# Pooled attention followed by a maxout feed-forward: third buffers for q, folds of v by four heads, prologue constants in later buffers, and a new order of all steps

## The chip, the cores and the metric

The kernel runs on one core of one Trainium2 chip. The core has TensorE (PE; its weight loads are shown as PEld), VectorE (DVE), ScalarE (ACT), GpSimd (POOL) and SyncE (SP). Each takes its instructions in the order in which the program issues them and waits at an instruction until the semaphores that it needs have been raised. The metric is the device time of one execution in microseconds (us); less is better. Three runs of the kernel before gave 227.71, 229.46 and 230.1 us, median 229.46.

## The reference

```python
# q, k, v: (8, 8, 576, 64) float32: batch, heads, sequence, head size
k_p = k.reshape(B, H, 72, 8, D).mean(axis=3)        # keys and values averaged over 8 neighbours
v_p = v.reshape(B, H, 72, 8, D).mean(axis=3)
scores = q @ k_p^T / sqrt(D)                        # 576 x 72 for each batch and head
attn = softmax(scores)
attn_out = attn @ v_p                               # (8, 8, 576, 64)
x = attn_out.transpose(0, 2, 1, 3).reshape(4608, 512)
h = max(max(x @ w1, x @ w2), x @ w3)                # 4608 x 768
out = h @ w_out                                     # 4608 x 512, float32
```

## The kernel before

**Tiling.** The attention goes batch by batch (8 batches b of 576 tokens, 8 heads), the feed-forward part by blocks n of 512 tokens (9 blocks). The transposed attention output is a ring `xT` of 2048 tokens, from which the blocks read, so that both parts run interleaved.

**Attention.** `load_q`, `load_k` and `load_v` (lines 89 to 115) load a batch from GpSimd's DMA queue into the pool `ld`, which has two buffers of each tile (`qb`, `ktFalse`, `vt`). Keys are pooled on VectorE in two additions (`pieces`, "k", lines 794 to 802; tiles `halfh`, `kp`) and turned by TensorE into `kz` (`turn_k`, line 207; `kz` is copied from PSUM by `move`). Values are folded in `pieces` (lines 803 to 814): four additions on GpSimd from `vt` into `half` (line 807, two heads each), two from `half` back into `vt` (line 811, four heads each), and one on VectorE into `vp`. q of batches 0 to 2 is transposed on TensorE (`turn_q`, line 187) and copied out of PSUM into `qT`; that of batches 3 to 7 by three DMA transposes on SyncE's queue (line 305). `scores_flat` (line 237) makes 512 columns of scores in a PSUM bank (`psf`, two of them) and ScalarE writes the exponentials to `et`. `values` (line 267) multiplies 128 tokens with `vp` into `pav` (one buffer), and VectorE divides by the sum (`rcp`, then `xn`, line 279). `turn_x` (line 250) brings `xn` into `xT`: for batches 0 to 2 through TensorE and PSUM, later by DMA transposes on SyncE's queue (line 256).

**Feed-forward.** The maximum of three products is written as max(x(w2-w1), x(w3-w1), 0) plus x w1, so that x w1 w_out becomes x times a matrix `wm` made once. Blocks 0 to 3 make plain products (`hidden`, `project`, `two_products`). For blocks 4 to 8 the hidden products, and for all blocks from 1 on the output products, are done in the form of seven half-size products for eight; they need sums of quarters on VectorE (`sum_t` and `sum_h`, line 596: tiles `xs`, `hs`; `fold_w` and `fold_out` for the weights: `sums`, `sw`, `soh`) and additions of the results (`hidden_product`, `out_product`). Results go through four PSUM banks `pb`, handed out by `take` and `give`. `move` (line 78) copies PSUM on ScalarE, or on VectorE where the step's name ends in a star. Stores go out on SyncE's queue (lines 421 and 692), those of the last block also on other queues.

**Order.** After a prologue (up to about 39 us in the profile) all is issued by `run` (line 829) from the string `ORDER` (line 879), step by step. The names: `qbi` transposes a part of q of batch b on TensorE, `Tb` issues the next of three DMA transposes of q, `sbj` makes a block of scores, `vbc` the values of 128 tokens (from batch 3 on with their transposes), `xbc` the transposes of batches 1 and 2, `Kb` and `Vb` the next piece of a fold, `kb` turns the keys, `<kb`, `<qb`, `<vb` load; `p` is a half of a first output tile; `f F S G` sums of weights, `t1..t4` and `u1..u4` sums of quarters; `A1..H4` plain hidden products; `1a..7c` hidden products and `1d..7d` output products of the seven.

Two additions of waits shape the queues. A load (`<`) waits for the latest matmul issued before it and for the latest DMA transpose issued before it (line 841). A GpSimd piece of a fold (`piece`, line 816) waits for the latest VectorE operation that was made through `both` (line 536), that is, one that works on SBUF alone.

Of the kernel before, what the change touches and what calls it, by code (L numbers as in the profile page):

```python
# [10 lines left out]
ALU = mybir.AluOpType  # L11
# [3 lines left out]
def kernel(  # L15
# [91 lines left out]
                for h, g in zip(cuts, cuts[1:])][-1]  # L107

    def load_q(b):
        qbs[b] = ld.tile([128, 4, NG, D], BF16, name="qb", tag="qb")  # L110
        src = q[b].rearrange("h s d -> (h s d)").rearrange(
            "(hp p t d) -> p hp t d", hp=4, p=128, t=NG)
        n = 2 if b == 0 else 4
        return [nc.gpsimd.dma_start(out=qbs[b][:, i:i + n], in_=src[:, i:i + n])
                for i in range(0, 4, n)][-1]
# [10 lines left out]

    load_q(0)
    load_k(0, nc.sync, F32, 3)
    warm = const.tile([128, 512], BF16, name="warm", tag="warm")
    nc.vector.memset(warm, 1.0)  # L130
    ident = const.tile([128, 128], BF16, name="ident", tag="ident")
    make_identity(nc, ident)
    identh = const.tile([128, 128], F16, name="identh", tag="identh")
    make_identity(nc, identh)
    load_v(0, nc.gpsimd, cuts=(0, 4, 8))
    pick = const.tile([96, 6, 128], F16, name="pick", tag="pick")
    nc.gpsimd.memset(pick, 1.0)
    for sign in (1, -1):
        nc.gpsimd.affine_select(
# [47 lines left out]

    def turn_q(b, n0, n1, evac, tag):
        if b not in qTs:
            qTs[b] = sb2.tile([128, 2 * NG, 128], BF16, name="qT", tag="qT")  # L190
        pqt = psum([128, n1 - n0, 128], BF16, name="pqt", tag=tag[0],
                       bufs=tag[1])
        qf = qbs[b].rearrange("p hp t d -> p (hp t d)")
        for n in range(n0, n1):
            transpose(pqt[:, n - n0, :], qf[:, 128 * n:128 * n + 128],
                                ident)
        evac(out=qTs[b][:, n0:n1, :], in_=pqt)
# [96 lines left out]
    def do(b, steps):  # L294

        for name in steps.split():
            i = int(name[1:] or 0)
            if name[0] == "q":  # L300
                turn_q(b, *QS[i], move, TR if len(pools) < 3 else SC)
            elif name[0] == "T":
                if i == 0:
                    qTs[b] = sb2.tile([128, 2 * NG, 128], BF16, name="qT", tag="qT")
                turned[:] = [nc.sync.dma_start_transpose(
                    out=qTs[b][:, 6 * i:6 * i + 6],
                    in_=qbs[b].rearrange("p hp t d -> p (hp t d)")[:, 768 * i:768 * i + 768])]
# [291 lines left out]

    def sum_h(n, i):  # L600
        if n not in ths:
            ths[n] = hs if n < LAST else const.tile([128, 4, JH, HALF], F16, name="hs8",
                                                    tag="half")
        sum_t(quads(n), ths[n], i)

    def bank(of, n, g):
# [184 lines left out]
    def pieces(what, b):  # L791

        t = (kts if what == "k" else vts)[b]
        if what == "k":
            new_kp(b)
            f = const.tile([96, 6, 4, D], F16, name="halfh", tag="k16")
            both(f, t[:, :, 0:4, :], t[:, :, 4:8, :], ALU.add)
            yield
            both(kps[b].rearrange("p j i d -> p i j d"), f[:, :, 0:2, :], f[:, :, 2:4, :],
                 ALU.add)  # L800
            yield
            return
        f = const.tile([Sp, H, 4, D], F32, name="half", tag="half")
        e = nc.gpsimd
        for i in range(0, H, 2):
            c = slice(i, i + 2)
            yield e.tensor_tensor(out=f[:, c], in0=t[:, c, 0:4, :], in1=t[:, c, 4:8, :],  # L807
                                  op=ALU.add)
        for i in range(0, H, 4):
            c = slice(i, i + 4)  # L810
            yield e.tensor_tensor(out=t[:, c, 0:2, :], in0=f[:, c, 0:2, :], in1=f[:, c, 2:4, :],  # L811
                                  op=ALU.add)
        both(vp_all[:, b % 3, :, 0:D], t[:, :, 0, :], t[:, :, 1, :], ALU.add)
        yield

# [84 lines left out]

    run(ORDER)
# [36 lines left out]
```

## Time and profile before

| | |
|---|---|
| Runs | 227.71, 229.46, 230.1 us; median 229.46 |
| The profiled execution | 227.75 us, span 225.9 us |
| TensorE clock granted, mean | 0.997 |
| DMA packets | 33.57 MB, mean 149 GB/s |
| 63 exponentials (ACT et<-psf) | 595 ns each |
| 28 first additions of v (POOL half<-vt) | 1189 ns each |
| 14 second additions of v (POOL vt<-half) | 1300 ns each |
| 40 divisions (DVE xn<-pav,rcp) | 691 ns each |
| Loads of q, k, v to landing, median | 9.5, 13.2, 14.1 us |

The page of the profile divides the span in 40 slices of 5.6 us; each digit is the busy share of an engine in a slice, in tenths:

```
PE   7788999899999999999998999996999999999991
DVE  3558967276999899987899965989989998988651
ACT  2267525687866887354369855957454571674230
POOL 7975300969419546459012027125140000000020
DMA  6999999989999799989999999995371541430085
```

In the rows of a timeline a line has start, duration, engine, line of the kernel, operation, out<-in and the count, and in brackets the idle time before it with what ended it. In the chain of waits a line has start, duration and the engine and tile that the end of the span depended on at that time.

### The profile page before, as it was taken

The numbers are of one execution on the slowest core, as the hardware profiler recorded it, in microseconds if no ns is written. First come the engines' busy times: TensorE is split into PE (matmuls) and PEld (weight loads), VectorE is DVE, ScalarE is ACT, GpSimd is POOL, SyncE is SP. The second block draws the span as 40 slices with busy tenths as digits, with TensorE's granted clock in tenths as the row PEclk, the third lists the DMA queues.
The fourth block names the chain that finished last, engine by engine and source line by source line (L and its number), as shares of the span: only waits on it lengthen the run. The fifth ranks groups of instructions, "written<-read, shape, count | busy, mean of one in ns | idle before, by whom it ended". The sixth has DMA issues, their size and how long they took to land.

```text
span 225.9 us, 5235 instructions
## 1 busy us (share of the span) xinstructions
PE 212.3 (94%) x2046; PEld 165.7 (73%) x2046; DVE 180.2 (80%) x362; ACT 132.0 (58%) x264; POOL 82.7 (37%) x90
## 2 busy tenths in 40 slices
PE   7788999899999999998999996999999999999991
PEld 2377745558986666874679885988989898888881
DVE  3558967276999899987899965989989998988651
ACT  2267525687866887354369855957454571674230
POOL 7975300969419546459012027125140000000020
PEclk9999999999999999999999999999999999999998
DMA  6999999989999799989999999995371541430085
GB/s 166 208 197 197 204 207 205 204 160 236 151 156 132 126 163 182 151 171 194 134 211 172 155 125 171 195 156 107 70 166 36 136 105 31 115 73 0 4 229 141
DMA packets 50824, 33.57 MB, mean 149 GB/s; under 512 B 27280, under 2 KB 46352, under 8 KB 50800
## 3 DMA queue, kind: packets, MB, share of 16 engines
q0 software_dynamic: 20304, 16.98, 51.6%
q1 hardware_dynamic: 30208, 16.00, 40.8%
q8 instruction: 16, 0.26, 0.5%
q10 hardware_dynamic: 288, 0.26, 0.4%
q14 instruction: 8, 0.07, 0.1%
HBM read 34.60 MB, written 9.44 MB: 195 GB/s over the span
## 4 chain that ended last, share of the span: by engine, by line
PE 73%; DVE 11%; DMA 9%; issue 3%; ACT 1%; POOL 1%; SPq 0%; POOLq 0%; DVEq 0%; ACTq 0%
PE pb L70 54%; PE psf L70 5%; DMA qT<-qb 5%; PE pw L70 4%; PE pav L70 4%; DMA vt<-in_v_dram 4%; DVE xn L279 3%; PE pm L70 2%; PE pxt L74 1%; DVE hT L682 1%; DVE xs L537 1%; PE oC L70 1%; DVE kz L78 1%; DVE hs L537 1%; DVE rcp L277 1%
## 5 line engine op out<-in xcount | busy, mean ns | idle before, releaser
L70 PE MATMUL pb<-xT,mw 128*128 128x256 f16 (+1 forms) x312 | 52.8, 305 | 1.2 <-DVE hT L682 1.2
L70 PEld LDWEIGHTS <-mw 128*128 128x128 f16 x444 | 41.5, 98 | 16.3 <-issue 2.2
L807 POOL TENSOR_TENSOR half<-vt 72x512 f32<-72x512 f16 x28 | 32.9, 1189 | 52.9 <-DMA vt<-in_v_dram 42.6
L226 ACT ACTIVATE et<-psf 72x512 f16<-72x512 f32 x63 | 35.3, 595 | 8.2 <-PE psf L70 8.1
L279 DVE TENSOR_TENSOR xn<-pav,rcp 128x512 f16<-128x512 f32 x40 | 27.7, 691 | 1.4
L78 ACT COPY osb<-pb 128x512 f32<-128x512 f32 x25 | 14.7, 587 | 23.7 <-PE pb L70 23.7
L70 PE MATMUL psf<-qT,kz 128*128 128x256 bf16 (+4 forms) x161 | 21.3, 249 | 2.6 <-DMA qT<-qb 2.0
L636 DVE TENSOR_TENSOR ys<-ys,pb 128x512 f16<-128x512 f16 x30 | 20.3, 682 | 2.3 <-PE pb L70 2.0
L70 PEld LDWEIGHTS <-kz 128*128 128x128 bf16 x185 | 14.6, 98 | 8.5 <-issue 3.4
L70 PEld LDWEIGHTS <-hs 128*128 128x128 f16 x192 | 18.8, 98 | 2.2
L811 POOL TENSOR_TENSOR vt<-half 72x512 f16<-72x512 f32 x14 | 18.0, 1300 | 5.9 <-DVE xs L537 3.4
L692 POOL DMA_DIRECT2D out_dram<-ob x2 | 1.3, 636 | 50.1 <-DVE ob L763 50.1
L70 PE MATMUL pb<-mwo,hT 128*128 128x256 f16 (+1 forms) x120 | 19.3, 294 | 0.0
L70 PE MATMUL pb<-soh,hs 128*128 128x256 f16 x138 | 19.1, 273 | 0.0
L70 PEld LDWEIGHTS <-hT 128*128 128x128 f16 x168 | 16.3, 98 | 3.6
L78 ACT COPY pb<-pb 128x512 f32<-128x512 f32 x21 | 12.0, 575 | 10.8 <-PE pb L70 7.0
L70 PE MATMUL pav<-vp,et 72*128 72x65 f16 x320 | 17.1, 194 | 0.8 <-DVE xn L279 0.4
L78 ACT CAST ys<-pb 128x512 f16<-128x512 f32 x27 | 15.6, 593 | 3.6 <-PE pb L70 3.3
L70 PE MATMUL pb<-xs,sums 128*128 128x256 f16 x90 | 17.2, 272 | 0.1
L70 PEld LDWEIGHTS <-et 72*128 72x128 f16 x320 | 14.6, 98 | 3.5 <-DVE xn L279 1.4
L70 PE MATMUL pb<-xs,sw 128*128 128x256 f16 x90 | 17.2, 272 | 0.0
L645 ACT ACTIVATE t<-pb 128x256 f16<-128x256 f32 x30 | 11.2, 387 | 8.2 <-PE pb L70 7.8
(111 smaller groups left out, 413.0 us busy)
## 6 DMA issues: line engine op xcount, KB each, us to landing
out_dram<-osb SPq DMA_DIRECT2D x38, 128.0 KB, 2.7
ktFalse<-in_k_dram POOLq DMA_DIRECT2D x7, 576.0 KB, 13.2
qb<-in_q_dram POOLq DMA_DIRECT2D x7, 576.0 KB, 9.5
vt<-in_v_dram POOLq DMA_DIRECT2D x7, 576.0 KB, 14.1
out_dram<-osb SPq DMA_DIRECT2D x13, 256.0 KB, 3.7
mw<-in_moe_w_dram POOLq DMA_DIRECT2D x9, 256.0 KB, 9.5
ktTrue<-in_k_dram SPq DMA_DIRECT2D x3, 384.0 KB, 5.5
mwo<-in_moe_w_out_dram POOLq DMA_DIRECT2D x1, 768.0 KB, 13.3
```

The lines of the kernel that those rows point to most:

```text
L70: latest[0] = nc.tensor.matmul(*args, **kw)
L74: latest[0] = nc.tensor.transpose(*args, **kw)
L78: (nc.vector.tensor_copy if on_vector[0] else nc.scalar.copy)(out=out, in_=in_)
L226: nc.scalar.activation(out=out, in_=in_, func=FT.Exp, scale=1.0 / 64.0)
L277: nc.vector.reciprocal(out=rcp, in_=pv[:, :, :, 64])
L279: nc.vector.tensor_tensor(out=xn, in0=pv[:, :, :, 0:D], in1=rcp.to_broadcast([128, 2, 4, D]), op=ALU.mult)
L537: t = e.tensor_tensor(out=out, in0=a, in1=b, op=op)
L636: nc.vector.tensor_tensor(out=y[:, j], in0=y[:, j], in1=bank("C", n, g), op=ALU.add)
L645: nc.scalar.activation(out=t0, in_=p[:, 0], func=FT.Relu)
L682: nc.vector.tensor_tensor(out=hTs[n][:, j, c], in0=relus[j], in1=b, op=ALU.max)
L807: yield e.tensor_tensor(out=f[:, c], in0=t[:, c, 0:4, :], in1=t[:, c, 4:8, :], op=ALU.add)
L811: yield e.tensor_tensor(out=t[:, c, 0:2, :], in0=f[:, c, 0:2, :], in1=f[:, c, 2:4, :], op=ALU.add)
```

## The change

Five things change.

- `qb` and `qT` have three buffers instead of two.
- `warm` and `pick`, constants of the prologue, are no longer in the pool `const`; they take a buffer of `t0` and of `kp`, which later steps use.
- `half`, the intermediate tile of the folds of v, holds four heads instead of eight. The six GpSimd additions of a batch are the same in kind and number; their order becomes two first additions, one second, two first, one second.
- `hs8`, the sums of the last block, was in the buffer of `half` and is now in one of `vt`.
- `ORDER` is new throughout. It has the same steps; six of the copies out of PSUM are starred that were not, and two no longer are.

```diff
--- before.py
+++ after.py
@@ -107,7 +107,7 @@
                 for h, g in zip(cuts, cuts[1:])][-1]
 
     def load_q(b):
-        qbs[b] = ld.tile([128, 4, NG, D], BF16, name="qb", tag="qb")
+        qbs[b] = ld.tile([128, 4, NG, D], BF16, name="qb", tag="qb", bufs=3)
         src = q[b].rearrange("h s d -> (h s d)").rearrange(
             "(hp p t d) -> p hp t d", hp=4, p=128, t=NG)
         n = 2 if b == 0 else 4
@@ -126,14 +126,14 @@
 
     load_q(0)
     load_k(0, nc.sync, F32, 3)
-    warm = const.tile([128, 512], BF16, name="warm", tag="warm")
+    warm = sb2.tile([128, 512], BF16, name="warm", tag="t0")
     nc.vector.memset(warm, 1.0)
     ident = const.tile([128, 128], BF16, name="ident", tag="ident")
     make_identity(nc, ident)
     identh = const.tile([128, 128], F16, name="identh", tag="identh")
     make_identity(nc, identh)
     load_v(0, nc.gpsimd, cuts=(0, 4, 8))
-    pick = const.tile([96, 6, 128], F16, name="pick", tag="pick")
+    pick = sb2.tile([96, 6, 128], F16, name="pick", tag="kp")
     nc.gpsimd.memset(pick, 1.0)
     for sign in (1, -1):
         nc.gpsimd.affine_select(
@@ -187,7 +187,7 @@
 
     def turn_q(b, n0, n1, evac, tag):
         if b not in qTs:
-            qTs[b] = sb2.tile([128, 2 * NG, 128], BF16, name="qT", tag="qT")
+            qTs[b] = sb2.tile([128, 2 * NG, 128], BF16, name="qT", tag="qT", bufs=3)
         pqt = psum([128, n1 - n0, 128], BF16, name="pqt", tag=tag[0],
                        bufs=tag[1])
         qf = qbs[b].rearrange("p hp t d -> p (hp t d)")
@@ -301,7 +301,7 @@
                 turn_q(b, *QS[i], move, TR if len(pools) < 3 else SC)
             elif name[0] == "T":
                 if i == 0:
-                    qTs[b] = sb2.tile([128, 2 * NG, 128], BF16, name="qT", tag="qT")
+                    qTs[b] = sb2.tile([128, 2 * NG, 128], BF16, name="qT", tag="qT", bufs=3)
                 turned[:] = [nc.sync.dma_start_transpose(
                     out=qTs[b][:, 6 * i:6 * i + 6],
                     in_=qbs[b].rearrange("p hp t d -> p (hp t d)")[:, 768 * i:768 * i + 768])]
@@ -599,8 +599,8 @@
 
     def sum_h(n, i):
         if n not in ths:
-            ths[n] = hs if n < LAST else const.tile([128, 4, JH, HALF], F16, name="hs8",
-                                                    tag="half")
+            ths[n] = hs if n < LAST else ld.tile([128, 4096], F16, name="hs8", tag="vt")[
+                :, 0:3072].rearrange("p (i k c) -> p i k c", i=4, k=JH)
         sum_t(quads(n), ths[n], i)
 
     def bank(of, n, g):
@@ -800,16 +800,15 @@
                  ALU.add)
             yield
             return
-        f = const.tile([Sp, H, 4, D], F32, name="half", tag="half")
+        f = const.tile([Sp, 4, 4, D], F32, name="half", tag="half")
         e = nc.gpsimd
-        for i in range(0, H, 2):
-            c = slice(i, i + 2)
-            yield e.tensor_tensor(out=f[:, c], in0=t[:, c, 0:4, :], in1=t[:, c, 4:8, :],
-                                  op=ALU.add)
         for i in range(0, H, 4):
-            c = slice(i, i + 4)
-            yield e.tensor_tensor(out=t[:, c, 0:2, :], in0=f[:, c, 0:2, :], in1=f[:, c, 2:4, :],
-                                  op=ALU.add)
+            for j in range(0, 4, 2):
+                c = slice(i + j, i + j + 2)
+                yield e.tensor_tensor(out=f[:, j:j + 2], in0=t[:, c, 0:4, :],
+                                      in1=t[:, c, 4:8, :], op=ALU.add)
+            yield e.tensor_tensor(out=t[:, i:i + 4, 0:2, :], in0=f[:, :, 0:2, :],
+                                  in1=f[:, :, 2:4, :], op=ALU.add)
         both(vp_all[:, b % 3, :, 0:D], t[:, :, 0, :], t[:, :, 1, :], ALU.add)
         yield
 
@@ -877,25 +876,25 @@
     for _ in range(SC[1]):
         psum([128, NB], F32, "psf", *SC)
     ORDER = """
-        q12* q13 V1 p s10 s11 p* s12 V1 s13 p s14 q20* s15 V1 s16 V1 V1 p* s17 V1 s18 K2 V1
-        <k3 p K2 q21 q22 <q3 V2 v10 V2 q23 V2 k2 v11 x10* <q4 p x11* v12 s20 p s21 V2 V2 V2
-        s22 v13 H3 <v3 s23 s24 <k4 v14 V3 C3 s25 f x13 f B3 T3 V2 K3 x12 T3 E3 T3 G s26 K3
-        s27 A4 V3 s28 t1 C4 T4 x14 v20 A3 S S T4 T4 D4 v21 x20 V3 D3 B4 x21 k3 v22 t3 u1 E4
-        H4 V3 V3 <v4 v23 x22 p S G A1 H1 V3 A2 v24 s30 s31 K4 1d s32 s33 H2 s34 C1 K4 <q5
-        x23* G s35 <k5 C2 t2 s36 s37 V3 t3 D1 t1 u2 s38 D2 k4 <v5 S u3 x24 G v30 E1 6d* V4
-        s40 s41 t2 B1 s42 t4 v31 V4 u4 s43 V4 B2 s44 v32 s45 5d s46 F v33 s47 E2 T5 s48 V4
-        V4 v34 7d u1 2d V4 V5 u3 <k6 K5 F V5 u2 3d 4d 1d K5 7d V4 t1 V5 2d <k7 6d* k5 v40 T5
-        C1 V5 t4 C2 s50 s51 v41 V5 V5 T5 E1 H1 E2 v42 <q6 H2 5d u4 f B1 F D1 V5 f D2 4d B2
-        K6 t2 K6 3d t3 A1 A2 F <v6 1a t1 1b <q7 s52 t2 u1 s53 v43 2a 2b K7 V6 s54 6b 6a s55
-        u3 K7 s56 v44 1d s57 t4 5a s58 V6 u2 V6 2d t3 t4 3a u4 v50 k7 7b 5b* 6d T6 v51 7a 3b
-        k6 4b T6 5d 4a T6 7d 1c T7 3d 2c 6c 4d t1 V6 V6 <v7 t2 5c T7 1a T7 v52 7c s60 s61 2a
-        3c s62 s63 6a v53 s64 4c 1b 5a s65 s66 v54 2b 3a s70 6b 1d s67 t3 u1 u2 u3 u4 t4 s68
-        5b 2d 7b V6 6d V6 V7 7a 4b 3b s71 v60 4a 1c 5d 6c* 2c s72 V7 v61 s73 7c s74 5c s75
-        7d s76 V7 v62 3c s77 4c t1 4d 3d t2 u1 1d t4 u2 V7 v63 s78 t3 1a 2d u3 2a 6a 1b* 6d*
-        2b v64 V7 V7 5a V7 6b 7a 3a 5d v70 5b 4a 7b v71 3b 3d u4 1c 4b 7d t1 t2 6c 7c 2c 5c
-        4d 3c 1a 4c v72 1b 2a 6a 6b u1 u2 2b 5a u4 t4 v73 1d 5b u3 3a t3 6d v74 3b 2d* 7b 7a
-        5d 4b 4a 7d t1 1c 3d 6c* 2c t3 4d t2 1a t4 5c 7c 2a 3c 6a 4c 1b 5a 7a 6b 2b 4a 5b 1c
-        u1 3a 3b 2c u2 6c u4 u3 1d 7b 5c 6d* 4b 3c 2d 5d 7c 7d 4c 3d 4d
+        q12* V1 V1 q13 p s10 s11 p* V1 s12 s13 p V1 q20* s14 q21* s15 s16 V1 V1 q22* K2 s17
+        <k3 <q4 s18 p V1 V2 <q3 K2 v10 q23* k2 V2 v11 F x10 p x11* s20 V2 v12 s21 D3 s22 V2
+        v13 x12 G A3 s23 s24 B3 V2 V2 x13 v14 <v3 t1 f <k4 t2 s25 V2 <v4 C3 s26 T3 s27 T3 G
+        A4 S s28 T3 V3 V3 T4 B4 V3 T4 T4 t4 x14 V3 v20 K3 p* V3 p v21 x20* K3 C4 E3 H3 V3
+        v22 u1 x21 k3 E4 D4 x22* v23 V4 H4 p D1 1d* K4 <k5 K4 B1 V4 D2 s30 S G s31 B2 S u2
+        t3 s32 k4 2d* s33 A1 <q6 s34 v24 s35 6d* s36 t1 V3 u4 u3 s37 <q5 H1 <k6 s38 5d f <v5
+        S V4 x23 v30 s40 A2 s41 v31 s42 H2 s43 s44 v32 V4 E1 s45 V4 t3 V4 t2 s46 v33 T5 E2
+        T6 x24 C1 s47 V4 K5 K5 V5 G <k7 s48 C2 7d k5 V5 u3 u1 3d u2 4d f v34 1d 7d v40 u4 K6
+        6d V5 2d v41 K6 t1 T5 F 5d H1 V5 k6 T5 H2 s50 T6 v42 t4 f A1 V5 s51 3d* A2 V5 4d D1
+        C1 D2 V5 <v6 C2 t2 <q7 <v7 F B1 B2 F 1a t1 E1 t2 t3 2a v43 K7 T6 s52 s53 6a 1b t4 t3
+        s54 E2 V6 s55 V6 u3 6b 5a s56 t4 v44 2b 5b s57 K7 7a s58 3a 3b s60 v50 1c u1 s61 4a
+        s62 1d u2 2c k7 6c v51 V6 2d 7c u4 T7 v52 T7 s63 5c 7b 6d 3c 4c v53 5d 7d V6 4b 3d
+        4d T7 u1 v54 1a 1d s64 u2 s65 t1 t2 2a 2d* s66 V6 s67 u3 6a 1b* s70 V6 V7 V6 6d u4
+        s68 t4 6b V7 t3 5a 2b 5d 3a v60 5b 3d 7b 7a V7 7d V7 s71 4a s72 4b s73 4d 1c 3b s74
+        V7 v61 t1 2c 1a 6c s75 v62 2a 5c t2 7c V7 s76 v63 3c 6a 1b 4c u1 5a t3 t4 s77 v64 6b
+        s78 2b 3a 5b u2 1d V7 3b 7a u3 2d v70 7b 4a 6d 4b v71 1c 5d u4 6c 7d v72 2c 5c* t1
+        t3 4d 3d v73 1a t2 3c 7c 2a 6a v74 1b 4c 5a t4 2b 6b 3a u1 1d u3 5b u2 7a 2d 3b 4a
+        6d 1c 7b u4 5d 6c t1 t2 4b 3d* 5c 7d 7c 2c 3c 4d 1a 4c 1b 2a t3 6a u1 6b u2 2b t4 5a
+        u4 1d 3a u3 5b 2d* 7a 3b 6d 4a 7b 1c 5d* 6c 4b 2c 3d 5c 7c 7d 4c 3c 4d
     """
 
     run(ORDER)
```

## The prediction

> **What bounds the kernel now.** I read the busy table and the chain first, then TensorE's busy time by stage, then the queues around each place where TensorE stands still.
>
> The page's first and fourth part (busy time; chain by engine):
> ```profile
> PE 212.3 (94%) x2046; PEld 165.7 (73%) x2046; DVE 180.2 (80%) x362; ACT 132.0 (58%) x264; POOL 82.7 (37%) x90
> PE 73%; DVE 11%; DMA 9%; issue 3%; ACT 1%; POOL 1%; SPq 0%; POOLq 0%; DVEq 0%; ACTq 0%
> ```
> TensorE sets the time, VectorE is second. The order comparison shows that the change removes no matmul, so only TensorE's stops can be won. Where they are, by stages (stretch and length, then busy us of PE, PEld, DVE, ACT, POOL, clock, DMA share, GB/s):
> ```profile
> 39.00:56.00 17.00, 15.92 (x159) 10.69 (x158) 9.62 (x21) 12.77 (x25) 14.64 (x14) 1.00 1.12 199
> 56.00:104.50 48.50, 47.00 (x466) 35.05 (x463) 45.41 (x85) 33.85 (x69) 27.45 (x26) 1.00 1.17 154
> 104.50:137.70 33.20, 31.21 (x295) 24.46 (x294) 26.37 (x53) 19.73 (x40) 8.44 (x9) 1.00 1.30 168
> 150.00:200.00 50.00, 49.90 (x515) 44.39 (x514) 46.84 (x95) 28.09 (x57) 7.05 (x6) 1.00 0.49 103
> ```
> From 39 us on TensorE idles 1.1 us in the first stretch, 1.5 in the second (VectorE is 94% busy there), 2.0 in the third and 0.1 in the fourth. Before 39 us the new order is the old one.
>
> The stop in the third stretch, in the chain in order of time (start, us, what):
> ```profile
> 126.84 0.32 SPq L256
> 127.25 10.34 DMA qT<-qb
> 137.64 0.60 PE psf L70 x5
> ```
> and its cause, on GpSimd's queue and on SyncE's:
> ```profile
> 117.54 0.78 POOL L114 DMA_DIRECT2D qb<-in_q_dram  x1 [10.36 <-PE pav L70]
> 127.25 1.71 SPq L305 DMA_TRANSPOSE qT<-qb  x1
> ```
> The load of batch 6's q leaves at 117.54, its first transpose (T6) at 127.25, lands at 137.6, and the scores s60 wait 1.99 us. The row names a values matmul; that had long ended. The load also waits for the latest DMA transpose ahead of it in the order, x42, issued at 111.56 (xT transposes land after 5.4 us, median: about 117).
>
> Why VectorE is so busy in the second stretch (VectorE, then GpSimd):
> ```profile
> 101.00 2.71 DVE L537 TENSOR_TENSOR xs<-xT,xs 128x512 f16<-128x512 f16 x1
> 100.63 2.27 POOL L807 TENSOR_TENSOR half<-vt 72x512 f32<-72x512 f16 x2
> ```
> The same xs addition takes 0.41 us alone; here it ends after two folds of v have run. Ten such additions between 56 and 104 us take together 8.65 us more than their shortest rows (for instance hs 1.51 for 0.54, halfh 2.03 for 0.94, soh 1.79 for 0.54). The Trainium skill, "SBUF — State Buffer", section "Who interferes with whom", says that of a GpSimd operation and such a VectorE operation whichever starts second fully blocks until the first is done; by that rule the trace agrees, this row even across two folds.
>
> **Scale used below.** "Matmul time" (mt) is the work of matmuls issued so far at the chain's pace, 0.86 to 0.88 us for eight of 256 columns; all matmuls come to 201 us mt. It tells how far apart two steps stand for TensorE in either order. On VectorE neighbouring operations overlap by 0.08 us, so I count each row less 0.08.
>
> **1. New order: batch 6's q.** The load moves from 94.7 to 65.1 us mt and T6's first part to 76.6, against s60 at 107.5: 31 us mt for a transpose that took 10.3; before it had 9.3. The 1.99 us stop goes: **-2.0**. What is late next there: the first T5 now leaves 13.3 us mt ahead of s50, the first T7 13.2 ahead of s70, the last T7 11.4 ahead of its reader; the longest landing was 14.2, the median 7.7. Load q5 now has 8.7 us mt to T5 where loads of q took 9.5 (median), so SyncE may stand 1 to 3 us, with T6 and the stores behind it; the stores' readers stand 4.7 us mt or more off, and a store lands in 2.7. Taken at 0; +2 if T5 lands as late as T6 did (range).
>
> **2. Queues moved past.** GpSimd carries loads and folds in one order. v3, k4 and v4 go out at 43.4, 46.3 and 48.4 us mt (42.8, 45.5 and 56.5 before) and wait for no late transpose; v6 and v7 at 96.6 and 101.1 (100.6 and 120.2). Every batch's folds end 1.5 to 10 us mt ahead of its values steps (1.4 to 12 before). k7 waits for T6's landing and holds one fold back about 6 us; that batch's values come 26 us mt later. Taken at 0.
>
> **3. The first values of batch 1 (v10).** In the chain:
> ```profile
> 45.86 0.04 DVE osb L78
> 46.47 0.94 DVE halfh L537
> 47.41 0.35 DVE vp L537
> 47.80 0.43 PE pav L70 x8
> ```
> GpSimd's folds of v1 run back to back from the landing at 39.41 to 46.34 and can't come earlier; folding by four heads leaves 4 x 1.14 + 2 x 1.27. In the new order v10 stands at 36.2 us mt, not 37.1: 0.9 us of other matmuls now come after it. vp can follow at 46.4 at best (v10 at 46.9: cost 0), but the fold of k2 (0.94) is queued ahead of vp and would start at about 45.5, inside the last fold of v; if it's held to 46.34 as xs was, vp ends at 47.6, and v10 starts as before with 0.9 less behind it. With the evacuation of q23 now on VectorE behind xn (0.42) the worst is +1.2. No gain is possible, since v1's landing holds. **+0.6**, the middle.
>
> **4. VectorE between v10 and the keys of batch 6.** Six evacuations move to VectorE and two away over the kernel: 0.49 + 2 x 0.42 (q) + 2 x 0.69 (osb) + 0.70 (pb) - 2 x 0.69 (ys) = 2.0 us, and others come earlier. From v10 to the end of T5 (88.2 us mt) the new order gives VectorE 44.7 us for 52.0 of matmuls; the old one 40.7 for 51.0. To this come the blocked additions. Pieces of v folds in the stretch: 21 instead of 24, at the old 8.65/24 each: 7.6, sum 52.3 (old: 49.4, and the stretch took 56.4). Counting instead, for each piece, what VectorE has to do between the addition that releases it and the next one that it can block: 15.5 us unhidden against 12.0, of which 8.65 came true; so 11.2, sum 55.9. Against 52 of matmuls VectorE is even with TensorE, where it was 2 us short. Fewer idle us (-1.5, all of the second stretch's idle) or more (+3.8, below) are both open. I take **0**: the piece count says less, the cover count more.
>
> **5. Short evacuation waits after 104 us.** Where a matmul waits for a copy, I took the mt between the copy's own matmul and the waiting one, less 0.25 us and the rows queued ahead. It falls short at 30 places in the old order after 104 us, by up to 0.32 (110.5, 122.3, 180.4 us mt; the chain leaves PE there, as for ys at 199.41), at about 10 in the new, by up to 0.23. Largest shortage of each run added up: 1.5 against 0.5. **-0.8**, between 0 and -1.0, as busy time shows only 0.2 of it.
>
> **6. At nothing.** The third buffers themselves: with two, T6 would wait for the last read of batch 4's qT, at 76.8 us mt, 0.2 after its place; T4 for batch 2's, 2.5 after, with 26 in hand; the loads of q for none. So the order, not the room, moves q. The warm-up tile in t0's buffer and the pick matrix in kp's: last read at 11 and 14 us, first overwritten after 20 and at 47; a moved owner would cost one tile wait there. hs8 in v's buffer: written at 214, v last read at 168. A half-size fold buffer adds one wait of GpSimd on itself per batch; such a wait exists now (L811 after L807, 43.85 after 43.89) and costs nothing measurable, at most 7 x 0.07.
>
> **Sum.** -2.0 + 0.6 + 0 - 0.8 = -2.2. The profiled execution has a span of 225.9 and a time of 227.75, so 225.6; it lies 1.7 under the median of the runs, 229.46 (227.71 to 230.1). On the median: **227.3**.
>
> **Rivals.**
> *VectorE becomes the bound (slower).* If every piece blocks as the cover count says, 15.5 us, v10 to T5 needs 44.7 + 15.5 = 60.2 instead of 56.4 for one more us of matmuls: +2.8 to +3.8. With +0.6 and -2.0: 231.9 at most. It decides from about 12 us of blocking on. It's the Trainium skill's rule of above with no piece finding cover. For it: 94% busy now, folds of v3 and v4 landing together. Against: VectorE's order put 30% of that cover to use before.
> *A wash.* The stop at s60 goes, +1.2 at v10, +0.6 of VectorE in the stretch, short waits unchanged: -0.2, 229.3. For it: all three are bounds of rows above.
> *All idle goes.* -2.0, 0 at v10, -1.5, -1.0: -4.5, 225.0. For it: loads are further ahead everywhere; against: item 3.
> *The buffers don't do what the change says.* That is item 6: no time by itself, and part of every case.
>
> **Numbers.** Forecast 0.48, all idle gone 0.17, wash 0.22, VectorE 0.13. A measurement of this kernel can tell about 1% from no change: 2.3 us. Below 227.2 lie the third case, over half of the first (its own range 225.3 to 229.3) and a little of the wash: 0.46. Above 231.7 most of the VectorE case and a late T5: 0.12. Between: 0.42. Range 223.6 to 231.4: it leaves out half of the VectorE case and the far end of the best one.
>
> **What would show it.** No wait of psf on qT; the first T6 issued before 95 us; v10 at 47 to 48 us with a stop before it; VectorE's long xs, hs, soh and halfh rows between 56 and 104 us summing to 7 to 11 us; TensorE over 98% busy after 104 us. I am wrong if blocked additions pass 12 us, if SyncE's stand on q5 reaches a store that an evacuation needs, or if v10 starts before 46.8.

## The result, and the profile after

| | before | after |
|---|---|---|
| Runs, median | 229.27 us (17 runs, 227.11 to 232.8) | 231.58 us (17 runs, 228.98 to 234.31) |
| The profiled execution: time, span | 227.75, 225.9 us | 230.71, 229.0 us |
| TensorE clock granted, mean | 0.997 | 0.989 |

The ratio of after to before is 1.010, 95% interval 1.006 to 1.014: slower by about 2.3 us, where 2.2 us less were forecast. The median lies 0.2 us above the top of the forecast's range, 231.4. Executions more than 1.5% above the fastest of their kernel (3 of 17 before, 4 of 17 after, 6 of 11 in e5, 8 of 12 in e10) are in the medians but in no ratio, here or below, and the profiles of e5, e6, e10, e11, e12 and e16 are of such executions.

The changed kernel's page, busy time and chain by engine, and two rows of its 40 slices:

```profile
PE 213.1 (93%) x2045; PEld 166.6 (73%) x2046; DVE 179.9 (79%) x366; ACT 129.1 (56%) x260; POOL 84.9 (37%) x90
...
PE   7688999889999999995999989999999999999991
...
PEclk9999999999999999999799999999999999999998
...
PE 70%; DVE 13%; DMA 5%; ACT 4%; issue 2%; POOL 1%; SPq 1%; DVEq 0%; POOLq 0%; ACTq 0%
```

DMA fell from 9 to 5% of the chain, ScalarE rose from 1 to 4. One slice of TensorE is down to 5, near 107 us, and the next has a clock of 7 tenths. The same stages as before:

```profile
39.00:56.00 17.00, 14.90 (x149) 10.05 (x148) 11.21 (x23) 12.21 (x25) 13.98 (x13) 1.00 1.06 184
56.00:104.50 48.50, 48.34 (x486) 36.53 (x484) 43.18 (x90) 30.07 (x62) 25.33 (x23) 1.00 1.16 170
104.50:137.70 33.20, 29.39 (x260) 21.36 (x258) 26.12 (x50) 22.05 (x46) 13.16 (x12) 0.95 1.08 168
150.00:200.00 50.00, 50.00 (x520) 44.90 (x519) 44.55 (x93) 29.48 (x61) 8.02 (x6) 1.00 0.41 79
```

TensorE idles 2.1 us in the first stretch (1.1 before), 0.2 in the second (1.5), 3.8 in the third (2.0), and in the third the clock is 0.95. To place it by work done, take the start of the matmul at a given matmul time, less that matmul time, in both traces; the difference of two such values is what was lost in between:

| matmul time, us | lost before | lost after | difference | predicted |
|---|---|---|---|---|
| to 28 | 9.31 | 9.68 | +0.4 | 0 |
| 28 to 55 (opening) | 2.90 | 4.30 | +1.4 | +0.6 (item 3) |
| 55 to 88 | 1.69 | 0.96 | -0.7 | 0 (item 4) |
| 88 to 112 | 1.62 | 5.09 | +3.5 | 0 (within item 1) |
| 112 to 124 (s60) | 2.60 | 1.43 | -1.2 | -2.0 (item 1) |
| 124 to 199 | 1.87 | 1.46 | -0.4 | -0.8 (item 5) |

The sum is +2.9 of the 3.1 us between the spans. Profiles of the kernels below with the same steps in a stretch show what of this is an accident of one execution. To 28 us they lose 8.9 to 9.5 us with either opening, so the 0.4 is none of the change. In the opening the new order loses 4.3 to 5.3 us, that of before 2.7 to 3.3: that row is firm. From 55 to 88 us both spread (0.9 to 3.5 us new, 1.6 to 4.6 old), and -0.7 says nothing. The 3.5 us are one stop. The changed kernel's timeline around it (start, us, engine, line, operation):

```profile
79.56 0.74 POOL L94 DMA_DIRECT2D ktFalse<-in_k_dram  x1 [1.49 <-PE psf L70]
81.40 1.53 POOL L114 DMA_DIRECT2D qb<-in_q_dram  x2
83.58 0.75 POOL L94 DMA_DIRECT2D ktFalse<-in_k_dram  x1 [0.64 <-PE psf L70]
84.32 0.85 POOL L106 DMA_DIRECT2D vt<-in_v_dram  x1
...
94.45 7.37 SPq L305 DMA_TRANSPOSE qT<-qb  x2
101.93 4.42 SPq L692 DMA_DIRECT2D out_dram<-osb  x7
...
102.65 1.44 POOL L808 TENSOR_TENSOR half<-vt 72x512 f32<-72x512 f16 x1 [12.09 <-DMA vt<-in_v_dram]
...
106.30 0.59 ACT L78 COPY osb<-pb 128x512 f32<-128x512 f32 x1 [4.59 <-DMA out_dram<-osb]
106.79 0.60 ACT L680 ACTIVATE t<-pb 128x512 f16<-128x512 f32 x1
...
107.28 1.95 ACT L78 CAST kz<-pkt 64x288 bf16<-64x288 f32 x4
107.44 1.50 PE L70 MATMUL pb<-xT,mw 128*128 128x512 f16 x4 [2.59 <-ACT t L680]
...
109.28 0.59 PE L70 MATMUL psf<-qT,kz 128*128 128x64 bf16 x3 [0.34 <-ACT kz L78]
```

Read it from below. TensorE stands 2.59 us for a relu of ScalarE and 0.34 for a kz copy. ScalarE had stood 4.59 us ahead of the relu, at the copy of product 5d of block 5 into `osb`: its buffer was still being stored. SyncE sent the seven stores of block 4 only at 101.93, though their last addition on VectorE ended at 96.87; ahead of them stood T5 and T6, 7.37 us of issuing. Far above, GpSimd sent five loads of 576 KB each from 79.56 to 84.32 (k5, q6, q5, k6, v5). They land one after the other, at 85.97, 89.50, 92.92, 96.91 and 102.49; the fold of v5 starts behind the last. In the kernel before only q5, k5 and v5 went out there, and v5 landed at 96.01. Its load and its seven stores, in the timeline of before:

```profile
81.86 0.85 POOL L106 DMA_DIRECT2D vt<-in_v_dram  x1 [1.81 <-PE pav L70]
...
96.78 4.90 SPq L692 DMA_DIRECT2D out_dram<-osb  x7
```

The first five of these stores landed 2.4 to 2.9 us after they were sent.

Windows of the changed kernel behind the stop (third from the right the granted clock):

```profile
106.00:108.00 2.00, 0.56 (x3) 0.31 (x3) 1.08 (x2) 1.69 (x4) 1.92 (x3) 0.96 0.75 115
108.00:110.00 2.00, 1.66 (x8) 0.73 (x7) 1.97 (x4) 1.95 (x5) 1.92 (x2) 0.50 1.00 214
110.00:112.00 2.00, 2.00 (x13) 1.36 (x12) 1.05 (x3) 0.81 (x2) 1.17 (x2) 0.69 1.22 203
```

The matmuls that follow the stop run at half the clock, from 107.85 to 111.26.

### The profile page after: what moved, and what is told of

Read it like the earlier page. It is cut to its first block, busy times and chain, and to the rows that moved or that the text cites. A ratio compares the mean times of both kernels' runs of the same rounds, so it can differ in the third digit from the quotient of the medians.

```text
span 229.0 us, 5238 instructions
## 1 busy us (share of the span) xinstructions
PE 213.1 (93%) x2045; PEld 166.6 (73%) x2046; DVE 179.9 (79%) x366; ACT 129.1 (56%) x260; POOL 84.9 (37%) x90
## 4 chain that ended last, share of the span: by engine, by line
PE 70%; DVE 13%; DMA 5%; ACT 4%; issue 2%; POOL 1%; SPq 1%; DVEq 0%; POOLq 0%; ACTq 0%
PE pb L70 52%; PE psf L70 4%; PE pw L70 4%; DMA vt<-in_v_dram 4%; PE pav L70 4%; DVE xn L279 3%; ACT kz L78 2%; PE pm L70 2%; DVE xs L537 2%; DVE hs L537 1%; DMA out_dram<-osb 1%; PE pxt L74 1%; DVE halfh L537 1%; PE oC L70 1%; DVE hT L682 1%
## 5 line engine op out<-in xcount | busy, mean ns | idle before, releaser
L808 POOL TENSOR_TENSOR half<-vt 72x512 f32<-72x512 f16 x28 | 35.0, 1257 | 58.7 <-DMA vt<-in_v_dram 40.9
L78 ACT COPY osb<-pb 128x512 f32<-128x512 f32 x23 | 13.5, 587 | 23.7 <-PE pb L70 18.2
L70 PE MATMUL psf<-qT,kz 128*128 128x256 bf16 (+4 forms) x161 | 22.2, 251 | 1.5 <-DVE qT L78 0.6
L70 PEld LDWEIGHTS <-kz 128*128 128x128 bf16 x185 | 15.1, 98 | 8.1 <-issue 3.3
L680 ACT ACTIVATE t<-pb 128x256 f16<-128x256 f32 (+1 forms) x24 | 11.6, 490 | 14.8 <-PE pb L70 13.3
L78 ACT CAST ys<-pb 128x512 f16<-128x512 f32 x29 | 16.8, 590 | 3.2 <-PE pb L70 2.8
L78 ACT COPY pb<-pb 128x512 f32<-128x512 f32 x20 | 11.5, 573 | 9.8 <-PE pb L70 7.2
```

The lines of the kernel that those rows point to most:

```text
L70: latest[0] = nc.tensor.matmul(*args, **kw)
L78: (nc.vector.tensor_copy if on_vector[0] else nc.scalar.copy)(out=out, in_=in_)
L680: nc.scalar.activation(out=relus[j], in_=a, func=FT.Relu)
L808: yield e.tensor_tensor(out=f[:, j:j + 2], in0=t[:, c, 0:4, :], in1=t[:, c, 4:8, :], op=ALU.add)
```

## The experiments

Theory and rivals at the start: the stop comes from SyncE's queue (A), from crowded DMA (B), or is only where slack of the whole order gathers (C). Ratios are to the kernel before, run on the same chip.

### Batch 6's first transpose out of the way

```diff
-v33 T5 E2 T6 x24 ... H2 s50 T6 v42
+v33 T5 E2 x24 ... H2 s50 T6 T6 v42
```

> The changed kernel with batch 6's first DMA transpose moved from ahead of x24 to beside its second (two steps named T6 after s50). Theory A (the stop at 104.5 to 109.3 us of the changed kernel comes from SyncE's queue: seven stores stand behind two slow transposes T5 and T6, 3.85 and 3.42 us, ScalarE's copy into osb waits for their landing, and relu, kz and TensorE wait behind that copy): the seven stores are issued about 3.4 us earlier, near 98.5, the copy's wait of 4.59 us falls to about 1.2, TensorE's stop of 2.59 us goes, and the granted clock stays at 1.00 at 108 to 112 us; time 3 to 4.5 us below the changed kernel's 231.6: 227 to 228.6. Theory B (the stores land late because loads and stores share the DMA engines; the queue is a bystander): stores issued earlier land at 105 to 107 as before, the copy still waits about 4 us, 231 to 232. Theory C (the time is lost to VectorE or to the new order as a whole, and the stop only collects slack): the stop goes and its time comes back behind it, 230.5 to 232.

Ratio 1.003 (0.997 to 1.008). The timeline of e1_t6_late:

```profile
98.19 5.54 SPq L692 DMA_DIRECT2D out_dram<-osb  x7
...
105.72 0.58 ACT L78 COPY osb<-pb 128x512 f32<-128x512 f32 x1 [3.67 <-DMA out_dram<-osb]
...
106.86 1.02 PE L70 MATMUL pb<-xT,mw 128*128 128x512 f16 x4 [1.66 <-ACT t L680]
...
108.69 0.38 PE L70 MATMUL psf<-qT,kz 128*128 128x64 bf16 x3 [0.81 <-ACT kz L78]
```

The stores are sent 3.7 us earlier, as A has it, but the copy starts only 0.6 us earlier, as B has it: the fourth store landed at 105.55 instead of 106.20. The stop shrinks from 2.59 to 1.66 us (the wait for a kz copy behind it grows from 0.34 to 0.81), the clock stays at 1.00, and the time fell with them, which speaks against C. So SyncE's queue alone was not it.

### Batch 5's first transpose out of the way too

```diff
-v33 T5 E2 T6 x24 ... t1 T5 F 5d
+v33 E2 x24 ... t1 T5 T5 F 5d
```

> As e1_t6_late, but batch 5's first transpose goes to its second too, so that neither stands ahead of the seven stores. Theory A: the stores are issued when their last addition ends, near 97 us, the copy's wait is gone, and little is gained over e1_t6_late (within 0.7 us of it) unless batch 5's transposes now come late for s50, which would show as a wait of psf on qT. Theory B: no change, 231 to 232. Theory C: 230.5 to 232.

Ratio 1.041 (1.030 to 1.052). All three theories missed it; only the "unless" of A named the place. The timeline of e1b_t5_t6_late:

```profile
114.49 0.58 PE L70 MATMUL psf<-qT,kz 128*128 128x320 bf16 x2 [8.80 <-DMA qT<-qb]
```

Batch 5's transpose, sent at 108.58 behind three xT transposes, landed at 114.45, and s50 stood 8.80 us. T5 had no room to move that far.

### The change without its order

```diff
-q12* V1 V1 q13 p s10 ...      (ORDER of the changed kernel)
+q12* q13 V1 p s10 s11 ...     (ORDER of before)
```

> All of the change but the order: three buffers of qb and qT, folds of v by four heads, the prologue's constants in later buffers, with the order of before. If the order alone made the changed kernel slower: as before, 229.3, within 0.6. If one of the other parts costs (GpSimd waiting on the half-size tile, a constant's buffer): 230 to 231.5, with the loss before 56 us for the constants or at the folds of v.

Ratio 0.996 (0.991 to 1.002), on five executions: buffers, folds and constants show no cost in the time. The loss is the order's.

### The same stop made by a short distance, by the burst, and by both

With e1 a theory D took the place of A and B: the five loads hold back all that is sent behind them, and 5d stands too few matmuls behind the stores whose buffer it takes. First, in the changed kernel, the distance (e11) and the burst (e9) taken away:

```diff
-t1 T5 F 5d H1 ... A1 V5 s51 3d*
+t1 T5 F H1 ... A1 V5 s51 5d 3d*
```

> The changed kernel with one output product, the 5d of block 5 whose copy into osb stood 4.59 us for the stores, moved from behind F to behind s51, some 5 us of matmuls later; loads, transposes and stores untouched. What the earlier runs left standing: with T6 out of the way the stores left SyncE 3.7 us earlier but landed only 0.5 us earlier, because all that was sent from 79.6 to 84.3 us (five loads of 1.2 MB or so, landing one after the other to 102.5) had to land ahead of them. Theory D (the stores land at 105 to 107 because of that burst, and 5d stands too few matmuls behind the stores whose tile it takes): the copy's wait falls below 0.5 us, TensorE's stop at 107 and the fall of the granted clock behind it go, and the time is 3 to 4.5 us under the changed kernel's: ratio to before 0.992 to 0.998. If the stop is slack that comes back at the next late thing (T5 for s50, x40's transpose): ratio 1.003 to 1.010.

Ratio 1.002 (0.997 to 1.007), between the two expectations; run again, below, for where the rest went.

```diff
-A1 <q6 s34 ... T5 E2 T6 x24 ... G <k7 s48 ... s50 T6 v42 ... 4d D1 ... K7 T6 s52
+A1 s34 ... T5 E2 x24 ... G <k7 <q6 s48 ... s50 v42 ... 4d T6 T6 T6 D1 ... K7 s52
```

> The changed kernel with the load of batch 6's q taken out of the burst (behind k7) and its three DMA transposes behind 4d. Theory D: v5, the last of the burst, lands near 99 instead of 102.5, GpSimd's fold of v5 starts as much earlier, the seven stores land near 102 to 103 and the osb copy waits 1 us or less; the stop of 2.59 us falls below 0.7: ratio to before 0.993 to 1.000, unless batch 6's q now comes late for s60 (a wait of psf on qT of 1 to 3 us: 1.000 to 1.010). If not the amount of loads but the order on SyncE's queue decides: stores land at 105 or later, ratio 1.003 or more.

Ratio 1.008 (1.002 to 1.014). The timeline of e9_q6_t6_late:

```profile
96.62 5.24 SPq L692 DMA_DIRECT2D out_dram<-osb  x7
...
97.63 1.15 POOL L808 TENSOR_TENSOR half<-vt 72x512 f32<-72x512 f16 x1 [6.49 <-DVE rcp L277]
...
102.50 0.58 ACT L78 COPY osb<-pb 128x512 f32<-128x512 f32 x1 [0.71 <-PE pb L70]
...
144.97 0.39 PE L70 MATMUL psf<-qT,kz 128*128 128x320 bf16 x2 [1.28 <-DMA qT<-qb]
...
152.25 0.60 PE L70 MATMUL pb<-sums,xT 128*128 128x256 f16 x4 [2.04 <-ACT osb L78]
```

v5 landed at 97.47, the first four stores by 101.80, the copy waits for no store and nothing stops at 107 (at 104.35 TensorE waits 1.03 us for kp). That part of D holds with e1 beside it, where the same stores went out 1.6 us later and the copy waited 3.67. But the loads behind go out later (v6, q7 and v7 from 125.4 on instead of 119.5), T7 has to wait for q7 until 141.23, and a stop for its transpose comes at 145 and another, for an osb copy, at 152: the time is about as bad as the changed kernel's.

Then, in the kernel before, the burst alone (e10), the distance alone (e12) and both (e13):

```diff
-K4 <q5 x23* ... v42 <q6 H2
+K4 <q5 <q6 x23* ... v42 H2
```

> The kernel before with the load of batch 6's q moved into its burst, right behind q5; nothing else. Theory D: k5 and v5 and the stores behind them land about 3.5 us later (v5 near 99.5 instead of 96.0), but before's osb copies stand 10 us of matmuls or more behind the stores of their tile, so no stop comes of it, and the wait of 1.99 us at s60 goes: ratio 0.988 to 0.995. If the burst costs wherever it is: a stop of 2 us or more between 92 and 106 us, ratio 1.000 to 1.010.

Ratio 1.000 (0.993 to 1.007), on four executions. No osb copy waits for a store, as D has it; v5 landed at 103.88, later than expected. In its profile, of an execution of 233.23 us, s60 has no stop of over 0.3 us, but psf waits 0.92 and 2.52 us for batch 5's qT at 120 and 124: there the gain went to batch 5.

```diff
-k5 v40 T5 C1 ... v42 <q6 H2 5d u4
+k5 v40 T5 5d C1 ... v42 <q6 H2 u4
```

> The kernel before with its 5d of block 5 moved up behind the first T5 after 4d, about as few matmuls behind the stores of block 4 as in the changed kernel. If the short distance alone makes the stop: a wait of the osb copy on the stores of 2 us or more near 101 us, and ratio 1.008 to 1.02. If distance and burst are both needed (theory D): the first four stores land within 3 to 5 us of their issue as now (by 101.5), the copy waits under 1 us, ratio 0.997 to 1.004.

Ratio 1.001 (0.995 to 1.006). The timeline of e12_5d_early_in_before, of an execution of 230.43 us whose granted clock was 0.95 throughout:

```profile
104.56 0.58 ACT L78 COPY osb<-pb 128x512 f32<-128x512 f32 x1
```

The copy of 5d has no wait; it comes right behind four kz copies, and the first four stores had landed by 103.88.

```diff
-K4 <q5 x23* ... k4 <v5 ... u3 <k6 K5 ... k5 v40 T5 C1 ... v42 <q6 H2 5d u4
+K4 <q5 <q6 x23* ... k4 <k6 <v5 ... u3 K5 ... k5 v40 T5 5d C1 ... v42 H2 u4
```

> The kernel before with 5d moved up as in e12_5d_early_in_before and, besides, the loads of q6 and k6 moved into the burst of q5, k5 and v5, so that five loads go out together as in the changed kernel. Theory D: the last of the five lands near 102, the stores behind them at 104 to 107, the copy of 5d waits 3 us or more, TensorE stands 2 us or more and its granted clock falls to 0.5 behind it; the s60 stop is gone (2.0 less): ratio 1.005 to 1.015. If the loss of the changed kernel needs something else of its order (VectorE, the opening): no stop, ratio 0.990 to 0.997.

Ratio 1.026 (1.019 to 1.034), worse than D gave, on three executions (a fourth took 442.69 us). The timeline of e13_5d_early_and_burst, then its windows:

```profile
105.79 3.37 POOL L807 TENSOR_TENSOR half<-vt 72x512 f32<-72x512 f16 x3 [9.40 <-DMA vt<-in_v_dram]
106.31 0.60 PE L70 MATMUL psf<-qT,kz 128*128 128x320 bf16 x5 [1.32 <-DMA qT<-qb]
107.94 0.58 ACT L78 COPY osb<-pb 128x512 f32<-128x512 f32 x1 [4.51 <-DMA out_dram<-osb]
...
109.08 5.28 PE L70 MATMUL pb<-xT,mw 128*128 128x512 f16 x12 [1.90 <-ACT t L680]
```

```profile
108.00:110.00 2.00, 0.92 (x3) 0.37 (x3) 1.45 (x3) 1.98 (x4) 1.99 (x4) 0.50 0.91 179
110.00:112.00 2.00, 2.00 (x6) 0.64 (x5) 0.99 (x3) 0.60 (x1) 2.00 (x2) 0.50 1.09 117
112.00:114.00 2.00, 2.00 (x6) 0.76 (x5) 0.00 (x0) 0.60 (x1) 1.45 (x2) 0.50 1.16 179
```

This is the changed kernel's stop in the order of before, by two moved loads and one moved product: the same copy waits 4.51 us for the same stores, TensorE for the same relu, and the clock halves. The product alone (e12) does not do it, nor does a burst that is as late alone (e10, with q6 but not k6 in it; e11 with all five in the changed order). With e9 that settles D as the cause of the stop. Beyond the forecast there are T5, which the burst delays as well (1.32 us), and a longer time at half clock; what share of the extra 1% each has is not shown.

### The opening

```diff
-V1 V1 q22* K2 s17 <k3 <q4 s18 p V1 V2 <q3 K2 v10
+V1 V1 q22* s17 <k3 <q4 s18 p V1 K2 V2 <q3 K2 v10
```

> The changed kernel with the first addition of k2's fold (halfh) moved behind the last piece of v1's fold, so that it no longer stands on VectorE ahead of vp. If halfh, 1.51 us there for 0.94 alone, holds v10 up as the prediction's third step put it: vp about 1.2 us earlier, v10 near 47.0 instead of 48.2, 0.6 to 1.2 us off the whole, ratio to before 1.004 to 1.008. If VectorE or the copies behind it catch up with that anyway: v10 earlier but the steps at 50 to 52 us no earlier, ratio 1.008 to 1.012.

Ratio 1.018 (1.004 to 1.032). halfh took 0.95 us instead of 1.51 and vp ended at 46.87 instead of 48.15, but v10 started at 47.57 and a wait of 0.69 for an xT copy on VectorE came at 52.79: at 55 us of matmul time 14.24 are lost, 13.98 in the changed kernel. The next addition is held up in its place: `sums` took 1.85 us from 50.54 on, 0.60 in the changed kernel, and the xT copy stands behind it.

```diff
-q12* V1 V1 q13 p s10 ... v14      (e11_5d_later)
+q12* q13 V1 p s10 s11 ... v14     (steps to v14 as before, the rest in the new order)
```

> As e11_5d_later, with the steps up to v14 in the order of before (q2's transposes apart, v10 after 0.9 us more of matmuls) and the rest in the new order. Theory: the opening of the new order costs about 1.4 us (v10 late with less done ahead of it, then four kz copies and an xT copy on ScalarE ahead of s22), and it stays: the time less matmul time at 55 us mt falls from about 14.1 to 12.5, ratio to before 0.991 to 0.998, under e11's 1.002. Rival: the opening's loss is made good by the stretch from 56 to 104 us in any case: ratio 0.999 to 1.005.

Ratio 1.011 (1.005 to 1.017). That is above both expectations. At 46 us of matmul time the old opening is 1.7 us ahead (11.89 lost, 13.61 in the changed kernel); at 58 it is 0.2 ahead (13.99 to 14.20), after 2.0 us lost between 46 and 52. The new order behind it does not keep what the old opening brings. Its profile has two stops further on, 1.63 us at 63.97 for xn and 1.52 at 78.25 for kp, that the changed kernel's does not have; whether the old opening causes them these runs don't show.

### The s60 stop by itself

```diff
-v41 V5 V5 T5 E1 H1 E2 v42 <q6 H2        (before)
+v41 V5 V5 <q6 T5 E1 H1 E2 v42 H2
```

> The kernel before with the load of batch 6's q moved ahead of the third T5, so that it no longer waits for the landing of x42's transpose; nothing else. If the stop of 1.99 us at s60 is worth what the prediction gave it: load issued near 114.4 instead of 117.5, T6 3 us earlier, stop gone, 227.3 (226.8 to 227.8). If another wait takes its place there, or T6 lands no earlier because the engines are crowded: 228.5 to 229.5.

Ratio 0.997 (0.993 to 1.001), but the load still went out at 119.39, held by the transpose ahead of it, so this tests nothing of s60.

```diff
-2d <k7 6d* ... v42 <q6 H2                (before)
+2d <k7 <q6 6d* ... v42 H2
```

> The kernel before with the load of batch 6's q right behind that of k7, ahead of the second T5 (e6_q6_early still waited there for a transpose: its load went out at 119.39). If the s60 stop is worth 2.0: load out near 104, T6 about 4 us earlier, stop gone, ratio 0.989 to 0.994. If the load crowds the transposes of batch 5 instead: a wait of psf for qT at s50 of 1 us or more, ratio 0.997 to 1.005.

Ratio 1.003 (0.998 to 1.007). The load went out at 103.11, s60 waited 0.33 us instead of 1.99, and batch 5 paid. The timeline of e15_q6_behind_k7:

```profile
119.32 0.54 PE L70 MATMUL psf<-qT,kz 128*128 128x320 bf16 x4 [2.93 <-DMA qT<-qb]
```

```diff
-1b <q7 s52 ... 6d T6 v51                 (before)
+1b s52 ... 6d T6 <q7 v51
```

> The kernel before with the load of batch 7's q moved behind the first T6, so that it no longer goes out right behind q6 and v6 (119.16 us) and lands ahead of that transpose (136.96 against 137.59). If what a transpose waits for is the loads sent ahead of it: T6 lands 3 to 6 us earlier, the s60 stop of 1.99 us is under 0.5, batch 7's q lands near 142 and its transposes still precede s70: ratio 0.988 to 0.995. If the stop only moves to batch 7: a wait of psf for qT at s70, ratio 0.997 to 1.003.

Ratio 1.025 (1.015 to 1.035). T6 went out at 128.46 and landed at 134.89, 6.4 us where it took 10.3 with q7 sent ahead of it, and the s60 stop is gone. The rival's place was right, its price far too low. The timeline of e17_q7_behind_t6:

```profile
144.15 1.21 SPq L305 DMA_TRANSPOSE qT<-qb  x1
...
146.98 0.61 PE L70 MATMUL psf<-qT,kz 128*128 128x320 bf16 x2 [4.54 <-DMA qT<-qb]
```

So what this transpose waits for are the loads sent ahead of it, and each place to which a load of q could be moved in the kernel before (e10, e15, e17) put the wait on another batch.

### What is late behind 5d

> The kernel of e11_5d_later once more, beside e16 on the same chip, for a profile of an undisturbed run. The question: 4.6 us of waiting went with 5d, but the ratio fell by only 0.008 (1.8 us). Theory D with no further loss: no stop above 0.5 us between 100 and 112 us, time less matmul time rises by under 1 us from 88 to 94 us mt (4.9 in the changed kernel), ratio 0.995 to 1.000. If batch 5's late transposes come next (psf on qT 0.78 us, kp 0.79, pb 0.84 in that profile): 1.5 to 2.5 us of the 4.9 stay, ratio 1.000 to 1.006.

Ratio 1.005 (1.001 to 1.009); with the first 1.002, 0.5 to 0.8% below the changed kernel. The timeline of e11_again:

```profile
106.90 0.38 PE L70 MATMUL psf<-qT,kz 128*128 128x320 bf16 x2 [1.51 <-DMA qT<-qb]
...
109.76 0.58 ACT L78 COPY osb<-pb 128x512 f32<-128x512 f32 x1 [0.24 <-PE pb L70]
110.39 0.60 PE L70 MATMUL pb<-sums,xT 128*128 128x256 f16 x4 [0.67 <-ACT osb L78]
```

The copy waits for no store. T5 comes next: it landed at 106.86 behind the same burst, and s50 waits 1.51 us. From 88 to 94 us of matmul time 2.8 us are lost, against 4.9 in the changed kernel and 1.3 before.

```diff
-T5 E2 T6 x24 ... F 5d H1 ... s50 T6 v42 ... s51 3d*
+T5 E2 x24 ... F H1 ... s50 T6 T6 v42 ... s51 5d 3d*
```

> The changed kernel with both 5d behind s51 and batch 6's first transpose behind s50. If the early T6 on SyncE's queue still costs something once 5d no longer waits (it holds the next xT transposes and batch 5's): 0.3 to 0.8 us under e11_again, ratio 0.993 to 0.999. If not: within 0.3 us of e11_again.

Ratio 1.002 (0.998 to 1.006). T5 landed at 105.46, psf no longer waits there, and 0.9 us are lost from 88 to 94. No kernel of these beats the one before beyond its interval; e5 (0.996) and e6 (0.997) come closest, e16 (1.002), e11 (1.002 and 1.005) and e1 (1.003) are the best in the new order.

## Why the prediction was wrong

**Item 1, the place that failed: "the stores' readers stand 4.7 us mt or more off, and a store lands in 2.7. Taken at 0".** The place was right and named as a way to be wrong, the cause and the price were not. SyncE never stood for q5: it landed at 92.92, and T5 began at 94.45, right behind the transpose ahead of it. The +2 of the range was for a late T5; T5 landed at 103.31, and no psf waits for it. What I missed are three things that act together. Issuing T5 and T6 takes 7.37 us, while the stores stand ready. The landing of 2.7 is a median over the whole kernel; where five loads are in flight, stores sent 3.7 us earlier land only 0.3 to 1.3 us earlier (e1: 98.19 to 103.79 for the first, 5.6 us). And 4.7 us of matmuls between the stores' last addition and their reader is short of both (e11, e13). Measured price: 3.5 us more than before in the table. Of the 5.1 lost there 2.9 are the two waits, and 3.4 us at half clock take up to 1.7 more.

The gain of the same item was right: psf waits for no qT of batch 6, the 1.99 us are gone. T6 left at 98.41, though, not before 95, because of the transposes queued ahead.

**Item 2, at 0.** The single waits were seen (k7 stood 1.45 us for T6's landing, where a fold was to be held back some 6). What it did not ask is what the loads do to each other: five in 4.8 us, 3.4 to 5.6 us each in line. The fault of item 1 begins here.

**Item 3, +0.6: too low.** halfh ran into the fold as feared (1.51 us for 0.94), but 1.4 us or more were lost, above the bound of 1.2. The chain of the changed kernel:

```profile
46.30 1.51 DVE halfh L537
47.81 0.35 DVE vp L537
...
48.20 0.42 PE pav L70 x8
...
49.14 0.47 ACT kz L78
...
51.12 0.60 ACT xT L78
...
51.75 0.38 PE psf L70 x2
```

Behind v10 four kz copies and an xT copy on ScalarE now end last; I had costed v10 alone. The blocked halfh is not what the opening costs: in e1 and the first e11 it took 1.00 and 0.97 us, and over 5 us were lost from 28 to 55 all the same. v10 itself stood only 0.07 us. Ahead of it TensorE waits 0.36 and 0.32 us for copies of q2's transposes and 0.32 for exponentials (before only 0.38, for exponentials), so that in e7 it comes to v10 0.7 us after vp is done. Which of these waits makes how much of the loss is open.

**Item 4, 0: stands, for another reason, and the VectorE rival is refuted.** TensorE idles 0.16 us in that stretch. The groups of VectorE in the changed kernel from 56 to 104 us (busy us, mean ns):

```profile
L537 DVE TENSOR_TENSOR halfh<-ktFalse 96x1536 f16<-96x1536 f16 x4 | 3.8, 946 | 0.0
...
L537 DVE TENSOR_TENSOR xs<-xT,xs 128x512 f16<-128x512 f16 x3 | 1.2, 410 | 0.0
```

Their means were 1306 and 1031 ns before. Means over the shortest rows add up to 2.7 us of blocking in this execution (sums 1.0, xs 0.5, hs and soh 0.4 each, sums again 0.4), not the 7.6 of the piece count or the 11.2 of the cover count. Neither count is of use without the times at which both engines come to the pieces.

**Item 5, -0.8: half of it.** 0.4 us from 124 us of matmul time on. Ahead of that, 1.3 us are lost anew at 112 to 118, where the chain runs over VectorE; they fall to 0.3 where the stop is smaller or gone (e11_again, e16, e9), so most of them seem to belong to the stop, though e1b, with 8.8 us of it, loses only 0.9 there.

**Item 6, at nothing: right for the time** (e5), though not for the folds: with a half-size tile each switch between first and second additions waits, and the fold of v1 takes 7.29 us (39.71 to 47.00) where it took 6.93, against 0.07 allowed. The span came to +3.1 instead of -2.2. The sum lacked the stop (3.5, with 1.3 behind it) and more than half of the opening.

Open: why a transpose of q takes up to 5.4 us of SyncE to issue, and what a better opening would need from the steps behind it.

## What to carry to other kernels

When a load is moved, list what else is sent to the DMA engines in the 20 us around it and let all land in line, each at what one takes in that place; then ask of every transpose and store behind them who reads it, and when. A reuse of a stored buffer needs its distance counted from when the queue reaches the store, not from when the data is ready. Removing a wait on a transfer by sending it earlier pays only where the place it moves to has room: here six moves of a q load or its transposes (the change, e1b, e9, e10, e15, e17) put a wait on another batch or on a store.

## What the runs showed of the hardware

The granted clock fell to 0.50 after some stops: for 3.41 us in the changed kernel (107.85 to 111.26), e5, e7 and e10, for 6.83 in e13 and e17 and for 10.24 in e1b. That is one, two or three times 3.41 us. Divide each trace into steps of that length, counted from where its clock first reaches 1.00 (5.45 us in the changed kernel; 107.85 is 30 steps later). In the step just before the fall TensorE had idled 2.3 us or more in all of these but e13. Stops of 2.93 us (e15) and 2.62 (e5, ending at 117.58) straddle two steps, with at most 1.6 us in either, and left the clock at 1.00; so did 1.9 us within one step (before, e1). In e13 1.7 us were enough, so idle time within a step does not decide alone either. The Trainium skill, "TensorE: Matmul & The Clock Gate", part 1, "What's actually happening", describes an activity window of some 3.4 us that runs freely. The lengths and places above agree with that; its statement that one idle window is needed does not cover these falls, as only e5 and e1b had a window without work.

A DMA transpose of q keeps SyncE for 1.3 us at the least and for up to 5.4 (changed kernel, median 2.28), so a row of them delays whatever that queue holds behind. Loads in flight are not the whole reason: with five of them in flight the first four transposes of `xT` took 1.2 to 1.5 us each, the fifth 2.95, and T5 and T6 behind them 3.85 and 3.42.
